# Attention's one-hot rows, AV groups and background steps rearranged in a fused attention and two-layer MoE kernel

## The chip, the cores and the metric

The kernel runs on one core of a Trainium2 chip. The metric is device time of one execution in microseconds (us); lower is better. The engines are PE (TensorE), DVE (VectorE), ACT (ScalarE), POOL (GpSimd) and SP (SyncE, which here only issues DMAs); each works through its own queue in the order in which the built program puts it.

## The reference

Sixteen heads (2 batches of 8) of 768 tokens and 64 dimensions. Every query and key is assigned to one of 16 centroids of its head; a score counts only where both have the same one. The result goes through two mixture-of-experts layers.

```python
q_assign = np.argmax(np.einsum('bhsd,hcd->bhsc', q_n, c_n), axis=-1)
k_assign = np.argmax(np.einsum('bhsd,hcd->bhsc', k_n, c_n), axis=-1)
mask = q_assign[:, :, :, None] == k_assign[:, :, None, :]
scores = scale * np.matmul(q, k.transpose(0, 1, 3, 2))
scores = np.where(mask, scores, -1000000000.0)
attn = np.exp(scores - np.max(scores, axis=-1, keepdims=True))
attn = attn / (np.sum(attn, axis=-1, keepdims=True) + 1e-09)
return np.matmul(attn, v)
```

Then `x` (1536 rows of 512) passes a layer whose tokens with `x @ w_skip > 0` go to the best of 8 experts, and a second layer in which all tokens do, each with an output gate. Expert weights are 512x1024 and 1024x512.

## The kernel before

**Attention**, from about 20 to 305 us of the span, is what the change touches. Heads are numbered 0 to 15 here, and each has six blocks `i` of 128 queries. The loop over `steps` does for block `i` of head `t`: the scores and the maximum of the block after it (`score`), its exponentials (`probs`), the work that belongs to this `i`, and the six transposes of its own exponentials (`flips`), which go through two PSUM tiles `tp` to the SBUF tile `PT`.

- `score` (L450 to 462) is four matmuls into one of two PSUM tiles `s`: two with QA and KA (L455), two with QB and KB (L457), then the negated row maximum on DVE (L461). QB and KB have 80 rows: 64 of data, and in rows 64 to 79 the one-hot assignment, which makes the mask by an added large negative number. So the second pair of a head's first score needs that head's one-hot rows.
- `dots`, `dots_sum` and `cluster` make the assignment of a later head: small matmuls into the free quarter of a `tp` tile (L420), their sums on DVE (L427), five small DVE steps (`first_max`). `one_hot` (L435) turns the result, 128 tokens by 16 clusters for each of six token groups, into rows by six transposes (L442) for the queries and six for the keys, and ACT copies them (L446, L448) into rows 64 to 79 of QB and KB.
- `av` (L479) multiplies `PT` with the values, six matmuls for each half of a head (three blocks). Matmul `k` writes 64 rows of the PSUM tile `o`, even `k` the lower and odd `k` the upper ones. `merge` (L491) projects and scales the half; after the last head of a batch it also writes 2 x 768 KB of rows to DRAM (L516).
- `load` and `split` fetch a head and split it into two parts; the split is five POOL instructions (L403 to L407).
- `split_weights` (L121) splits one eighth of the first expert's weights in each of heads 1 to 8: a copy on ACT (L135), and a subtraction on DVE (L138) when `flush_late` is called.
- `bg.step(2)` runs two steps of the generators that route batch 0 while batch 1 is in attention (heads 8 and later), small DVE instructions and a few matmuls.

The order on each engine is not the program's own: in attention a scheduler places the instructions by readiness and priority when the program is built, and the engines then keep that order. The MoE part behind attention is scheduled by hand and is not touched.

Of the kernel before, what the change touches and what calls it, by code (L numbers as in the profile page):

```python
# [35 lines left out]
def as32(ap):  # L36
    return ap.bitcast(F32)
# [3 lines left out]
def fused_kernel(ctx: ExitStack, tc: tile.TileContext, qT, kT, v, cN, wg, w11, w12, w21, w22, out):  # L41
    nc = tc.nc
    X = nc.dram_tensor("x_rows", (N, DM), F32, kind="Internal").ap()
    X2 = nc.dram_tensor("x2_rows", (N, DM), F32, kind="Internal").ap()

    const = ctx.enter_context(tc.tile_pool(name="const", bufs=1))
    wA = ctx.enter_context(tc.tile_pool(name="wA", bufs=1))
# [24 lines left out]
    def late_constants(pool):  # L72
        nc.gpsimd.memset(onesb, 1.0)
        nc.gpsimd.affine_select(out=trib, in_=onesb, pattern=[[1, 128]], compare_op=ALU.is_gt, fill=0.0, base=0, channel_multiplier=-1)
        for t in (TB1, TB2, base1, base2, LG2):
            nc.gpsimd.memset(t, 0.0)
        nc.sync.dma_start(out=wg2, in_=wg[:, 9:25].rearrange("(c p) g -> p c g", p=128))
        return (iota_f(pool, "io128", 128, [[1, 128]], 0, 0), iota_f(pool, "io12", NA, [[1, NA]], 0, 0),
                iota_f(pool, "d8", E, [[-1, E]], E, 0), iota_f(pool, "tok1", NA, [[128, NA]], 1, 1))
# [31 lines left out]
    def flush_late():  # L111
        for fn in [late.pop(0) for _ in range(len(late))]:
            fn()
# [273 lines left out]

    def split(t):

        if t >= NH:  # L390
            return
        qp, kp, vp = raw.pop(t)
        QA = spl.tile([128, S], F32R, tag="QA", name="QA")
        KA = spl.tile([128, S], F32R, tag="KA", name="KA")
        QB = spl.tile([80, S], F32R, tag="QB", name="QB")
        KB = spl.tile([80, S], F32R, tag="KB", name="KB")
        if t == 0:
            nc.scalar.copy(out=KA[:], in_=kp)
# [30 lines left out]
    def cluster(t, n):  # L429
        if t >= NH:  # L430
            return
        for _ in range(n):
            next(clus[t][0])

    def one_hot(t, s):  # L435
        if t >= NH:
            return
        oh = clus[t][1]
        T = ops[t][2 + s]
        po = ps_o.tile([80, S], BF16, tag="o", name="po") if s == 0 and t == 0 else ps_m.tile([80, S], BF16, tag="misc", name="po")  # L440
        for j in range(NJ):
            nc.tensor.transpose(out=po[64:80, 128 * j:128 * j + 128], in_=oh[:, s * NJ + j], identity=identb)  # L442
        if s == 0 and t == 0:
            nc.vector.tensor_copy(out=T[64:80], in_=po[64:80])
        elif s == 0:
            nc.scalar.copy(out=T[64:80], in_=po[64:80])  # L446
        else:
            nc.scalar.activation(out=T[64:80], in_=po[64:80], func=AF.Copy, scale=BIG, bias=-BIG)  # L448

    def score(t, i):  # L450
        QA, KA, QB, KB, _ = ops[t]
        sl = slice(128 * i, 128 * i + 128)
        s = ps_s.tile([128, S], F32, tag="s", name="s")
        for n0, n1 in ((0, 512), (512, S)):
            nc.tensor.matmul(out=s[:, n0:n1], lhsT=QA[:, sl], rhs=KA[:, n0:n1], start=True, stop=False)  # L455
        for n0, n1 in ((0, 512), (512, S)):
            nc.tensor.matmul(out=s[:, n0:n1], lhsT=QB[:, sl], rhs=KB[:, n0:n1], start=False, stop=True)  # L457
        if i == 0:
            sums[t] = asm.tile([128, NJ], F32, tag="rs", name="rs", bufs=2)
        mx = asm.tile([128, 1], F32, tag="mx", name="mx", bufs=4)  # L460
        nc.vector.tensor_reduce(out=mx, in_=s, axis=AX.X, op=ALU.max, negate=True)  # L461
        return s, mx

    def probs(t, i, s, mx):
        pr = prb.tile([128, S], F32, tag="pr", name="pr")
        nc.scalar.activation(out=pr, in_=s, func=AF.Exp, bias=mx, accum_out=sums[t][:, i:i + 1])  # L466
        return pr

    def flip(i, pr, PT, c):
# [90 lines left out]
    nc.vector.tensor_tensor(out=chl[:, :, 1], in0=c3, in1=as32(chl[:, :, 0]), op=ALU.subtract)  # L560

    split(0)
    load(1)
    split(1)
    d16 = iota_f(asm, "d16", NCL, [[-1, NCL]], NCL, 0)
    load(2)
    for c in (2, 1, 0):
        dp = ps_t.tile([128, 4, 128], F32, tag="tp", name="dp0")[:, 0].rearrange("p (t s) -> p t s", t=4)
        dots(0, c, dp)
        dots_sum(0, c, dp)  # L570
    cluster(0, 5)
    one_hot(0, 1)
    one_hot(0, 0)


    G = asm.tile([128, H, D + NG], F32, name="G")
    for p in (LO, HI):
        nc.sync.dma_start(out=G[p, :, D:], in_=wg.rearrange("(h d) g -> d h g", d=D))
        nc.gpsimd.tensor_scalar(out=G[p, :, 0:D], in0=ident[p, p].unsqueeze(1).to_broadcast([64, H, D]), scalar1=1.0, scalar2=1.0, op0=ALU.mult, op1=ALU.mult)
    io128, io12, d8, tok1 = late_constants(asm)  # L580

    wsets = [w_tiles(wA, "A"), None]
    wdone = 0
    def flips(t, i, pr, hook=None):

        for c in range(2):
            tp, dst = flip(i, pr, PT[t, i // 3], c)
            if hook and c == 0:
                hook(tp)
            if c == 0 or i % 2 == 0:  # L590
                nc.scalar.copy(out=dst, in_=tp[:, 0:3])  # L591
            else:
                nc.vector.tensor_copy(out=dst, in_=tp[:, 0:3])

    steps = [(t, i) for t in range(NH) for i in range(NJ)]
    cur = score(0, 0)
# [6 lines left out]
    for g, (t, i) in enumerate(steps[:-1]):  # L603
        half = i // 3
        if i % 3 == 0:
            PT[t, half] = ptb.tile([128, NJ, 384], F32, tag="PT", name="PT")
        old = pr
        cur = score(*steps[g + 1])
        pr = probs(*steps[g + 1], *cur)
        if i == 0:  # L610
            if t:
                av(t - 1, 1, PT[t - 1, 1], 0, 4)
            load(t + 3)
            split(t + 2)
            cluster(t + 1, 1)
        elif i == 1:
            if t:
                av(t - 1, 1, PT[t - 1, 1], 4, 6)
            cluster(t + 1, 1)
        elif i == 2:  # L620
            if t == NH - 1:
                first_turn()
            if t:
                merge(t - 1, 1)
                if t == H:
                    bg.add(route1(lg[0], 0, ps_m, asm, None, 2))
                    bg.add(first_tile())
                    bg.add(route_skip(lg[0], tok1[:, 0:NJ], ps_m, asm, 2))
            cluster(t + 1, 1)
        elif i == 3:  # L630
            one_hot(t + 1, 0)
            av(t, 0, PT[t, 0], 0, 2)
            if 1 <= t <= 8:
                if t == 1:
                    fetch(False, 2)
                split_weights(t - 1, False, False)
        elif i == 4:
            flush_late()
            one_hot(t + 1, 1)
            av(t, 0, PT[t, 0], 2, 6)  # L640
        elif i == 5:
            merge(t, 0)

        def hook(tp):
            if i > 2 and t + 2 < NH:
                dp = tp[:, 3].rearrange("p (t s) -> p t s", t=4)
                dots(t + 2, i - 3, dp)
                dots_sum(t + 2, i - 3, dp)

        flips(t, i, old, hook)  # L650
        if i == 0 or i == 1:
            cluster(t + 1, 1)
        if i > 1:
            bg.step(2)
    bg.drain()
    tl = NH - 1

# [621 lines left out]
```

## Time and profile before

| | |
|---|---|
| median of 3 runs | 724.88 us (724.53 to 724.91) |
| profiled execution | 725.64 us, span 723.9 us |
| mean granted TensorE clock | 0.969 |
| PE busy | 661.9 us (91%) |
| DVE busy | 464.0 us (64%) |
| ACT busy | 416.0 us (57%) |
| POOL busy | 185.2 us (26%) |

The span is the time from the first to the last instruction of the profiled execution; its own time is 1.7 us more. PE's matmuls overlap in the records, so the time that a group takes is best read as the start of the next group less its own start. A float32 matmul of four passes has two records, so that "x4" at an AV group is two matmuls of the program.

### The profile page before, as it was taken

Reading aid. Unit: us, or ns where it says so; the run is one execution under the profiler, and the core shown is the slowest. Engines: PE = TensorE matmul, PEld = TensorE weight load, DVE = VectorE, ACT = ScalarE, POOL = GpSimd, SP = SyncE. Lnnn points to the kernel's source line nnn. Section 1 sums busy time; section 2 is a strip of 40 time slices with the busy share of each in tenths; the row PEclk is TensorE's granted clock in tenths of the full one; section 3 lists DMA queues with packets and bytes.
Section 4 is the critical chain, followed back from the end, with each engine's and each line's share of the span. In section 5 each row is a group of like instructions: output and inputs, shape, how many; then the busy total and the mean of one; then the engine's idle time right before and its main releaser. Section 6 shows DMA issues by size and latency. Waiting matters only on the chain. (4 is left out here: it accounts for less than half of the span.)

```text
span 723.9 us, 12161 instructions
## 1 busy us (share of the span) xinstructions
PE 661.9 (91%) x4346; PEld 528.3 (73%) x4346; DVE 464.0 (64%) x964; ACT 416.0 (57%) x801; POOL 185.2 (26%) x193
## 2 busy tenths in 40 slices
PE   3999999998999999988988987988997999999995
PEld 2776667766667776766876876876875888899784
DVE  4667766668776667448767797857645755665520
ACT  1678877776566677535546766545534755555420
POOL 5544344433224310104211211201032022103011
PEclk9999999999899999989999999898899999999999
DMA  6747533347123102156637887727634576666200
GB/s 170 177 114 175 168 106 90 87 123 226 42 55 102 26 3 91 71 210 202 225 96 272 279 263 273 227 75 275 199 126 153 178 262 235 221 196 223 70 7 29
DMA packets 46554, 110.78 MB, mean 153 GB/s; under 512 B 7218, under 2 KB 9266, under 8 KB 46448
## 3 DMA queue, kind: packets, MB, share of 16 engines
q1 hardware_dynamic: 41536, 95.60, 42.5%
q0 software_dynamic: 4912, 13.88, 5.9%
q8 instruction: 52, 0.85, 0.5%
q14 instruction: 54, 0.44, 0.2%
HBM read 92.05 MB, written 13.24 MB: 145 GB/s over the span
## 5 line engine op out<-in xcount | busy, mean ns | idle before, releaser
L461 DVE TENSOR_REDUCE mx<-s 128x1 f32<-128x768 f32 x96 | 91.6, 955 | 30.7 <-PE s L457 26.9
L466 ACT ACTIVATE pr<-s,mx 128x768 f32<-128x768 f32 x96 | 86.8, 905 | 32.0 <-DVE mx L461 31.2
L473 PE MATMUL tp<-ident,pr 128*128 128x128 f32 x576 | 94.7, 289 | 5.0 <-ACT PT L591 4.4
L473 PEld LDWEIGHTS tp<-ident,pr 128*128 128x128 f32 x576 | 63.8, 145 | 42.7 <-ACT PT L591 18.5
L485 PE MATMUL o<-PT,vp 128*64 128x384 f32 x384 | 83.2, 512 | 0.2
L591 ACT COPY PT<-tp 128x384 f32<-128x384 f32 x144 | 65.7, 480 | 30.3 <-PE tp L473 23.6
L681 POOL DMA_INDIRECT xg<-x_rows,gi x33 | 38.8, 1177 | 110.6 <-DVEq L1134 39.2
L455 PE MATMUL s<-KA,QA 128*128 128x512 f32 x192 | 60.8, 393 | 3.6 <-DVE QA L401 3.4
L705 PE MATMUL ph<-w1hA,xt 128*128 128x256 f32 x208 | 54.1, 324 | 8.6 <-DVEq L1134 4.9
L457 PE MATMUL s<-KB,QB 80*128 80x512 f32 x192 | 53.4, 356 | 1.1 <-ACT KB L448 1.1
L705 PE MATMUL py<-w2hA,hh 128*128 128x512 f32 x112 | 47.9, 428 | 2.8 <-DVE hh L779 2.8
L705 PE MATMUL py<-w2hB,hh 128*128 128x512 f32 x112 | 46.6, 416 | 3.4 <-DVE hh L779 3.4
L705 PEld LDWEIGHTS ph<-w1hA,xt 128*128 128x128 f32 x208 | 40.4, 214 | 12.7 <-issue 10.4
L705 PE MATMUL ph<-w1hB,xt 128*128 128x256 f32 x192 | 43.8, 300 | 4.8 <-DVEq L1134 2.3
L705 PE MATMUL py<-w2lA,hh 128*128 128x512 f32 x112 | 47.5, 424 | 0.0
L705 PE MATMUL py<-w2lB,hh 128*128 128x512 f32 x112 | 46.3, 413 | 0.0
L817 DVE SCALAR_TENSOR_TENSOR hl<-phw,hh 128x256 fp32r<-128x256 f32 x48 | 20.2, 421 | 35.7 <-ACT hh L816 35.7
L485 PEld LDWEIGHTS o<-PT,vp 128*64 128x64 f32 x384 | 23.6, 138 | 25.6 <-issue 18.5
L338 DVE TENSOR_TENSOR xt<-tp,xt 128x512 fp32r<-128x512 f32 (+1 forms) x32 | 21.8, 681 | 29.6 <-ACT xt L337 25.2
L705 PE MATMUL ph<-w1lA,xt 128*128 128x256 f32 x128 | 40.4, 336 | 0.0
L816 ACT ACTIVATE hh<-phw 128x256 fp32r<-128x256 f32 x48 | 18.5, 385 | 37.5 <-PE phw L705 36.1
L138 DVE TENSOR_TENSOR w2lA<-raw,w2hA 128x1024 fp32r<-128x1024 f32 x32 | 39.1, 1227 | 0.2 <-ACT w2hA L135 0.2
(237 smaller groups left out, 1692.9 us busy)
## 6 DMA issues: line engine op xcount, KB each, us to landing
raw<-w SPq DMA_DIRECT2D x128, 512.0 KB
kp<-kT SPq DMA_DIRECT2D x32, 192.0 KB
qp<-qT SPq DMA_DIRECT2D x32, 192.0 KB
x_rows<-xb SPq DMA_DIRECT2D x8, 768.0 KB
vp<-v SPq DMA_DIRECT2D x16, 192.0 KB
KB<-KA SPq DMA_DIRECT2D x16, 192.0 KB
QB<-QA SPq DMA_DIRECT2D x16, 192.0 KB
xg<-x_rows,gi POOLq DMA_INDIRECT x33, 5.1
```

Of the source, the lines that this page charges most:

```text
L138: nc.vector.tensor_tensor(out=lo, in0=src, in1=as32(hi), op=ALU.subtract)
L338: nc.vector.tensor_tensor(out=lo, in0=tp, in1=as32(hi), op=ALU.subtract)
L455: nc.tensor.matmul(out=s[:, n0:n1], lhsT=QA[:, sl], rhs=KA[:, n0:n1], start=True, stop=False)
L457: nc.tensor.matmul(out=s[:, n0:n1], lhsT=QB[:, sl], rhs=KB[:, n0:n1], start=False, stop=True)
L461: nc.vector.tensor_reduce(out=mx, in_=s, axis=AX.X, op=ALU.max, negate=True)
L466: nc.scalar.activation(out=pr, in_=s, func=AF.Exp, bias=mx, accum_out=sums[t][:, i:i + 1])
L473: nc.tensor.transpose(out=tp[:, kk], in_=pr[:, 128 * k:128 * k + 128], identity=ident)
L485: nc.tensor.matmul(out=po[r:r + 64, :], lhsT=vp[:, k, :], rhs=PT[:, k, :], start=(k < 2), stop=(k >= NJ - 2))
L591: nc.scalar.copy(out=dst, in_=tp[:, 0:3])
L681: nc.gpsimd.indirect_dma_start(out=xg, out_offset=None, in_=src, in_offset=bass.IndirectOffsetOnAxis(ap=gi, axis=0))
L705: nc.tensor.matmul(**kw)
L817: nc.vector.scalar_tensor_tensor(out=ht[1][:, f, :], in0=ph, scalar=0.0, in1=as32(ht[0][:, f, :]), op0=ALU.max, op1=ALU.subtract)
```

## The change

1. One-hot rows. `one_hot` (for heads 1 to 15) now makes two transposes, one for queries and one for keys, each of 128 tokens by all 96 columns (6 groups x 16 clusters). ACT copies both into an SBUF tile `st`; one DMA writes `st` to a DRAM buffer, and two DMAs read it back into rows 64 to 79 of QB and KB. All three are in SP's queue. Head 0 keeps six and six (`one_hot0`).
2. The cluster steps are taken earlier, two at block 0, two at block 1, the last at block 2 together with `one_hot`.
3. AV is asked for as one group of six per half, at block 1 and block 4, where it was 4 and 2, and 2 and 4.
4. `behind` runs a piece of the program with an ordering edge: its DVE instructions are queued behind the newest block's maximum, and its ACT instructions behind that block's exponentials. It is order only, no wait. The weight splits and the background steps go through it, the latter now at every block.
5. The sums of the dots are placed behind the copy of their `tp` tile, and the loads of heads 1 and 2 and the split of head 1 behind head 0's one-hot rows.

```diff
-    def one_hot(t, s):
+    def one_hot(t):
...
+        oh = clus[t][1].rearrange("p j c -> p (j c)")
+        po = ps_m.tile([NJ * NCL, 2, 128], BF16, tag="misc", name="po")
+        st = asm.tile([NJ * NCL, 2, 128], F32R, tag="st", name="st", bufs=2)
+        for s in range(2):
+            nc.tensor.transpose(out=po[:, s], in_=oh[:, NJ * NCL * s:NJ * NCL * (s + 1)], identity=identb)
+        nc.scalar.copy(out=st[:, 0], in_=po[:, 0])
+        nc.scalar.activation(out=st[:, 1], in_=po[:, 1], func=AF.Copy, scale=BIG, bias=-BIG)
+        slot = OH[t % 2]
+        nc.sync.dma_start(out=slot.rearrange("s r t -> r s t"), in_=as32(st[:]))
+        for s in range(2):
+            nc.sync.dma_start(out=as32(ops[t][2 + s][64:80]).rearrange("c (j t) -> c j t", j=NJ), in_=slot[s].rearrange("(j c) t -> c j t", c=NCL))
+    def behind(fn):
+        with tc.issue_after(paced["DVE"]), tc.issue_after(paced["ACT"]):
+            fn()
...
-        nc.vector.tensor_reduce(out=mx, in_=s, axis=AX.X, op=ALU.max, negate=True)
+        paced["DVE"] = nc.vector.tensor_reduce(out=mx, in_=s, axis=AX.X, op=ALU.max, negate=True).ins
...
     split(0)
-    load(1)
-    split(1)
     d16 = iota_f(asm, "d16", NCL, [[-1, NCL]], NCL, 0)
-    load(2)
...
     io128, io12, d8, tok1 = late_constants(asm)
+    load(1)
+    split(1)
+    load(2)
...
         if i == 0:
-            if t:
-                av(t - 1, 1, PT[t - 1, 1], 0, 4)
             load(t + 3)
             split(t + 2)
-            cluster(t + 1, 1)
+            cluster(t + 1, 2)
         elif i == 1:
             if t:
-                av(t - 1, 1, PT[t - 1, 1], 4, 6)
-            cluster(t + 1, 1)
+                av(t - 1, 1, PT[t - 1, 1], 0, 6)
+            cluster(t + 1, 2)
...
             cluster(t + 1, 1)
+            one_hot(t + 1)
         elif i == 3:
-            one_hot(t + 1, 0)
-            av(t, 0, PT[t, 0], 0, 2)
             if 1 <= t <= 8:
                 if t == 1:
                     fetch(False, 2)
-                split_weights(t - 1, False, False)
+                behind(lambda: split_weights(t - 1, False, False))
         elif i == 4:
-            flush_late()
-            one_hot(t + 1, 1)
-            av(t, 0, PT[t, 0], 2, 6)
+            behind(flush_late)
+            av(t, 0, PT[t, 0], 0, 6)
...
-        flips(t, i, old, hook)
-        if i == 0 or i == 1:
-            cluster(t + 1, 1)
-        if i > 1:
-            bg.step(2)
+        flips(t, i, old, hook, after)
+        behind(lambda: bg.step(2))
```

What it makes of the built order stands at three places. Numbers at the names count tiles; they differ between the two programs.

PE, the second half's AV group of a head (tile `o`, L485 before and L505 now), at the change to the next head. Before:

```order
L455 MATMUL s_1651<-KA_1185,QA_1184 128x512
L455 MATMUL s_1651<-KA_1185,QA_1184 128x256
L485 MATMUL o_1613<-PT_1487,vp_736 64x384 x4
L473 MATMUL tp_1639<-ident_61,pr_1575 128x128 x3
L473 MATMUL tp_1644<-ident_61,pr_1575 128x128 x3
L457 MATMUL s_1651<-KB_1187,QB_1186 128x512
L457 MATMUL s_1651<-KB_1187,QB_1186 128x256
L485 MATMUL o_1613<-PT_1487,vp_736 64x384 x2
```

PE, the same place now:

```order
L493 MATMUL tp_1556<-ident_61,pr_1496 128x128 x3
L475 MATMUL s_1562<-KA_1152,QA_1151 128x256
L505 MATMUL o_1613<-PT_1461,vp_717 64x384
L477 MATMUL s_1525<-KB_1154,QB_1153 128x512
L477 MATMUL s_1525<-KB_1154,QB_1153 128x256
L477 MATMUL s_1562<-KB_1154,QB_1153 128x512
L477 MATMUL s_1562<-KB_1154,QB_1153 128x256
L505 MATMUL o_1613<-PT_1461,vp_717 64x384 x5
```

The six matmuls stand as one and five, where they stood as four and two. The one-hot rows are first needed by the second pair of `s_1525`. Over the whole program the groups of AV were 28 of two, 28 of four, 9 of one and 5 of three matmuls; now they are 27 of one, 27 of five, 3 of six, 2 of three and one each of two and four.

DVE, at block 4 of one of heads 1 to 8 (L138 and L139 are the weights' subtraction, `dt` the sums of the dots, which free a `tp` tile). Before:

```order
L461 TENSOR_REDUCE mx_1272<-s_1267 128x1
L427 TENSOR_REDUCE dt_1296<-tp_1288 128x64
L138 TENSOR_TENSOR w2lA_268<-raw_1757,w2hA_267 128x1024
L593 COPY PT_1266<-tp_1300 128x3x128
L461 TENSOR_REDUCE mx_1310<-s_1305 128x1
L427 TENSOR_REDUCE dt_1296<-tp_1331 128x64
```

DVE, the same place now:

```order
L613 COPY PT_1461<-tp_1484 128x3x128
L481 TENSOR_REDUCE mx_1494<-s_1489 128x1
L139 TENSOR_TENSOR w2lA_268<-raw_1071,w2hA_267 128x1024
L428 TENSOR_REDUCE dt_1480<-tp_1472 128x64
L428 TENSOR_REDUCE dt_1480<-tp_1510 128x64
L517 RECIPROCAL rr_1644<-rr_1644 128x3
```

The first sum of the dots now stands behind the maximum of the head's last block and behind the subtraction; all eight subtractions stand so. The block's transposes into `tp_1510` use the buffer that this sum frees, and on PE they stand right behind the first half's group of five.

SP, at the end of batch 0 (head 8), where `x_rows` and `x2_rows` are the 768 KB writes of `merge`, and `one_hot` the rows of head 9:

```order
L536 DMA x_rows<-xb_470 128x3x512
L536 DMA x2_rows<-xb_470 128x3x512
L459 DMA one_hot<-st_2087 96x2x128
L385 DMA qp_2226<-qT 64x768 x2
L461 DMA QB_1795<-one_hot 16x6x128
L461 DMA KB_1796<-one_hot 16x6x128
```

Before, this queue had no one-hot rows. In other heads the three DMAs stand together.

## Rows read from the trace of the kernel before

**Rows 1.** Windows: stretch, its length, busy time of each engine, PEclk, DMA share, GB/s.

```profile
140.00:160.00 20.00, 20.00 (x150) 15.23 (x149) 12.90 (x29) 14.26 (x34) 9.94 (x10) 1.00 0.37 97
...
168.00:171.00 3.00, 3.00 (x24) 2.01 (x22) 2.35 (x10) 2.95 (x8) 0.17 (x1) 1.00 0.93 345
```

**Rows 2.** Timeline of PE: start, duration, line, operation; one-hot transposes and AV groups.

```profile
100.59 0.50 PE L442 MATMUL po<-identb,oh 128*16 128x128 bf16 x6
101.03 0.86 PE L485 MATMUL o<-PT,vp 128*64 128x384 f32 x2
101.82 0.55 PE L473 MATMUL tp<-ident,pr 128*128 128x128 f32 x3
...
111.33 1.51 PE L485 MATMUL o<-PT,vp 128*64 128x384 f32 x8
112.77 0.87 PE L473 MATMUL tp<-ident,pr 128*128 128x128 f32 x6
...
113.69 0.87 PE L485 MATMUL o<-PT,vp 128*64 128x384 f32 x4
114.49 0.87 PE L473 MATMUL tp<-ident,pr 128*128 128x128 f32 x6
```

**Rows 3.** Timeline of PE: the first half's merge in heads 7 to 10, and a wait.

```profile
158.10 0.80 PE L500 MATMUL pf<-G,ot 128*128 128x89 f32 x6
...
174.72 0.80 PE L500 MATMUL pf<-G,ot 128*128 128x89 f32 x6
178.16 0.90 PE L473 MATMUL tp<-ident,pr 128*128 128x128 f32 x3 [2.63 <-ACT PT L591]
...
198.27 0.80 PE L500 MATMUL pf<-G,ot 128*128 128x89 f32 x6
...
218.46 0.80 PE L500 MATMUL pf<-G,ot 128*128 128x89 f32 x6
```

**Rows 4.** Timelines of POOL and DVE in the routing of head 8.

```profile
175.53 1.79 POOL L407 TENSOR_TENSOR QA<-qp,QA 64x768 fp32r<-64x768 f32 x1
...
175.66 1.74 DVE L286 TENSOR_TENSOR gz<-lg,goh 128x48 f32<-128x48 f32 x1
```

**Rows 5.** Timeline of PE: a score's first pair with its second half apart.

```profile
32.25 0.48 PE L455 MATMUL s<-KA,QA 128*128 128x512 f32 x1
32.56 0.51 PE L420 MATMUL tp<-chl,QA 128*128 128x32 f32 x4
```

**Rows 6.** Timelines of PE and DVE: a score, its maximum; a subtraction and a sum.

```profile
164.99 0.59 PE L455 MATMUL s<-KA,QA 128*128 128x512 f32 x2
165.42 0.52 PE L457 MATMUL s<-KB,QB 80*128 80x512 f32 x2
...
165.97 0.96 DVE L461 TENSOR_REDUCE mx<-s 128x1 f32<-128x768 f32 x1
...
87.15 1.53 DVE L138 TENSOR_TENSOR w2lA<-raw,w2hA 128x1024 fp32r<-128x1024 f32 x1
88.97 0.29 DVE L427 TENSOR_REDUCE dt<-tp 128x64 f32<-128x128 f32 x1 [0.29 <-PE tp L420]
```

**Rows 7.** Group of lines by form: the subtraction of the first weight matrix, set A.

```profile
L138 DVE TENSOR_TENSOR w1lA<-raw,w1hA 128x1024 fp32r<-128x1024 f32 x32 | 38.5, 1217 | 0.6 <-ACT w1hA L135 0.4
```

**Rows 8.** Timelines of SP and its waiters: two transfers from issue to use.

```profile
0.82 0.39 SPq L539 DMA_DIRECT2D c<-cN  x1
...
2.52 0.61 DVE L542 TENSOR_TENSOR csq<-c 128x64 f32<-128x64 f32 x1 [2.52 <-DMA c<-cN]
...
8.44 0.59 SPq L384 DMA_DIRECT2D kp<-kT  x1
...
11.99 0.84 POOL L403 TENSOR_SCALAR KA<-kp 128x768 fp32r<-128x768 f32 x1 [6.71 <-DMA kp<-kT]
```

**Rows 9.** Timeline of PE at the start: what stands ahead of the first transposes.

```profile
20.76 1.29 PE L420 MATMUL dp<-chl,QA 128*128 128x32 f32 x6
...
23.31 1.54 PE L473 MATMUL tp<-ident,pr 128*128 128x128 f32 x6
```

More of the change, by code (lines that the diff above doesn't have):

```diff
@@ L44, in fused_kernel @@
     X2 = nc.dram_tensor("x2_rows", (N, DM), F32, kind="Internal").ap()
+    OH = nc.dram_tensor("one_hot", (2, 2, NJ * NCL, 128), F32, kind="Internal").ap()
     const = ctx.enter_context(tc.tile_pool(name="const", bufs=1))
@@ L433, in cluster, with one_hot0 @@
             next(clus[t][0])
-    def one_hot(t, s):
+    def one_hot0(s):
+        oh = clus[0][1]
+        T = ops[0][2 + s]
+        po = ps_o.tile([80, S], BF16, tag="o", name="po") if s == 0 else ps_m.tile([80, S], BF16, tag="misc", name="po")
+        for j in range(NJ):
+            nc.tensor.transpose(out=po[64:80, 128 * j:128 * j + 128], in_=oh[:, s * NJ + j], identity=identb)
+        if s == 0:
+            nc.vector.tensor_copy(out=T[64:80], in_=po[64:80])
+        else:
+            nc.scalar.activation(out=T[64:80], in_=po[64:80], func=AF.Copy, scale=BIG, bias=-BIG)
+    def one_hot(t):
         if t >= NH:
             return
[L438 to L448, printed above, removed]
+        oh = clus[t][1].rearrange("p j c -> p (j c)")
[9 more added lines that the diff above has]
+            nc.sync.dma_start(out=as32(ops[t][2 + s][64:80]).rearrange("c (j t) -> c j t", j=NJ), in_=slot[s].rearrange("(j c) t -> c j t", c=NCL))
+    paced = {}
+    def behind(fn):
+        with tc.issue_after(paced["DVE"]), tc.issue_after(paced["ACT"]):
+            fn()
     def score(t, i):
@@ L465, in probs @@
         pr = prb.tile([128, S], F32, tag="pr", name="pr")
-        nc.scalar.activation(out=pr, in_=s, func=AF.Exp, bias=mx, accum_out=sums[t][:, i:i + 1])
+        paced["ACT"] = nc.scalar.activation(out=pr, in_=s, func=AF.Exp, bias=mx, accum_out=sums[t][:, i:i + 1]).ins
         return pr
@@ L571, in fused_kernel @@
     cluster(0, 5)
-    one_hot(0, 1)
-    one_hot(0, 0)
+    one_hot0(1)
+    one_hot0(0)
     G = asm.tile([128, H, D + NG], F32, name="G")
@@ L580, in fused_kernel, with flips @@
     io128, io12, d8, tok1 = late_constants(asm)
+    load(1)
+    split(1)
+    load(2)
     wsets = [w_tiles(wA, "A"), None]
     wdone = 0
-    def flips(t, i, pr, hook=None):
+    def flips(t, i, pr, hook=None, after=None):
         for c in range(2):
@@ L593, in flips @@
                 nc.vector.tensor_copy(out=dst, in_=tp[:, 0:3])
+            if after and c == 0:
+                after(tp)
     steps = [(t, i) for t in range(NH) for i in range(NJ)]
@@ L635, in fused_kernel, with after @@
                     fetch(False, 2)
-                split_weights(t - 1, False, False)
+                behind(lambda: split_weights(t - 1, False, False))
         elif i == 4:
-            flush_late()
-            one_hot(t + 1, 1)
-            av(t, 0, PT[t, 0], 2, 6)
+            behind(flush_late)
+            av(t, 0, PT[t, 0], 0, 6)
         elif i == 5:
             merge(t, 0)
+        dp = []
         def hook(tp):
             if i > 2 and t + 2 < NH:
-                dp = tp[:, 3].rearrange("p (t s) -> p t s", t=4)
-                dots(t + 2, i - 3, dp)
-                dots_sum(t + 2, i - 3, dp)
-        flips(t, i, old, hook)
-        if i == 0 or i == 1:
-            cluster(t + 1, 1)
-        if i > 1:
-            bg.step(2)
+                dp.append(tp[:, 3].rearrange("p (t s) -> p t s", t=4))
+                dots(t + 2, i - 3, dp[0])
+        def after(tp):
+            if dp:
+                dots_sum(t + 2, i - 3, dp[0])
+        flips(t, i, old, hook, after)
+        behind(lambda: bg.step(2))
     bg.drain()
```

## The prediction

> **What bounds the kernel now.** I read the windows first. In the steady stretch of attention PE is busy all 20.00 of 20 us, while DVE, ACT and POOL have slack [rows 1]; so every microsecond of matmul time put in or taken out counts there, and DVE counts only where PE waits for it. Then PE's timeline, for what its groups cost. The AV matmuls write alternating halves of one tile, and the starts show that neighbours run side by side: a group of one takes 101.82 − 101.03 = .79 us, a group of two 114.49 − 113.69 = .80, a group of four 112.77 − 111.33 = 1.44 (x8 records) [rows 2]. A group therefore costs about .15 plus .64 for each started pair; what counts is where groups are cut. Then the same timeline for waits. From one merge to that of the next head it is 174.72 − 158.10 = 16.62 us, in the next two heads 23.55 and 20.19 [rows 3]; those are heads 8 and 9, where the routing of batch 0 sets in. There PE waited 2.63 us for a copy of exponentials at 178.16 [rows 3], at a time when a routing instruction on DVE, tiny in size, took 1.74 us beside a POOL instruction of 1.79 that began just before it [rows 4].
>
> **AV.** The built order asks for 6 per half but gets 27 groups of one and 27 of five. Before: 28 x .80 + 28 x 1.44 + 9 x .79 + 5 x 1.43 = 77.0 us (three priced like four). Now: 27 x .79 + 27 x 2.08 + 3 x 2.08 + 2 x 1.43 + .80 + 1.44 = 88.8. No row shows five or six; 2.08 is my estimate, 1.44 + .64. **+11.8 us.** A lone matmul and a fifth one have no partner, and PE has no slack there to hide it. The one row for a lone matmul has transposes behind it; now the scores of the next head stand there, so its price lies between .15 and .79. I take .79, the measured one.
>
> **One-hot rows.** Thirty groups of six transposes at 101.03 − 100.59 = .44 us [rows 2] go: 13.2 us. Fifteen groups of two come, each at least .15 (a group's overhead above) and at most .44; I take .2, a third of .44 and a little, so 3.0. **−10.2** (−10.9 to −6.6). The two ACT copies take the place of twelve small ones and are covered: ACT has a third of its time free [rows 1].
>
> **Scores.** In the new order some 30 more first or second pairs have their two halves apart, with other work between them. A whole pair takes .43 (164.99 to 165.42 [rows 6]), a first half alone .31 (32.25 to 32.56 [rows 5]), and the second half, with half the columns, .15 (half of .31) to .31; so a cut costs .03 to .19. I take .08: **+2.4** (.9 to 5.7). PE's own work thus grows by 11.8 − 10.2 + 2.4 = 4.0 us.
>
> **Routing steps.** Behind the maximum they no longer delay a block's maximum or the copies that PE waits for. Heads 8 and 9 hold 23.55 + 20.19 − 2 x 16.62 = 10.5 us over the steady period [rows 3]. About 1 of it (an estimate from the routing's few small matmuls) stays. Of the other 9.5, what is late next is the `PT` copy of the same block, for a routing step behind the maximum still stands ahead of it, and a step can still meet POOL's split. I leave 2 (0 to 5): **−7.5**.
>
> **Weights' subtraction.** It now stands between the last block's maximum and the first sum of the dots, and PE's transposes wait for that sum's `tp` buffer. From the start of the score's second pair: .55 to the maximum (165.42 to 165.97), .96 for it, 1.53 for the subtraction beside POOL (87.15), .29 for the sum [rows 6]: 3.33. PE has meanwhile the rest of that pair, .4, and the group of five, 2.08: 2.5. PE waits .8 in each of eight heads: **+6.4**. Without POOL beside it a subtraction takes 1.22 (38.5 us for 32, [rows 7]), so .5 x 8 = 4 below; if it waits out a POOL instruction like that of 1.79 [rows 4], some 1.4 more, 2.2 x 8 = 17.5 above; and nothing, if PE comes to the place later than I think. I take the row at that place.
> The Trainium skill ("SBUF — State Buffer", Who interferes with whom) says that a DVE instruction with two SBUF inputs contends with a GpSimd instruction that reads SBUF, and that the first to issue holds the shared port for its whole duration. The rows' 1.74 beside 1.79 agrees; by the rule each subtraction could cost a whole split step, which would make the sum 11.1 larger.
>
> **One-hot rows through DRAM.** The three DMAs lie in SP's queue, mostly together, ahead of nothing that is urgent in steady heads. Two transfers in a row, each between 2.52 − .82 = 1.7 us and 11.99 − 8.44 = 3.55 from issue to use [rows 8], with transposes .2, copies .5 to 1 (an estimate, no row shows them) and a second issue at .4 to .6 [rows 8]: 4.5 to 8.9 us. In the order, some nine us of PE's work stand between the transposes and the second score pair that needs the rows. So hidden, at **0**, in steady heads; without the cover each head would pay what is missing. Head 9 is different: half of the batch's 2 x 2 row writes stands just ahead, and 4 x 393 KB = 1.57 MB at the 345 GB/s of the busiest window [rows 1] is 4.6 us in front. I take **+3** (0 to 7, the most that a head of [rows 3] lost).
> The Trainium skill ("DMA: Bandwidth & Descriptors", Anatomy of one DMA — SWDGE (gpsimd) path) puts the fixed cost of a transfer at about 2 us, mostly completion, and warns of surprisingly long delays when the target is HBM. No row of this kernel shows such a write being waited for; two such costs alone would be 4, hidden.
>
> **Start.** Dots of 2.55 us stood ahead of the first transposes (20.76 to 23.31 [rows 9]), in time in which PE waited for exponentials anyway. Now a score that needs a free tile stands there, and the split of head 1 on POOL and its loads on SP come later. **+1** (−1.5 if the dots just move out of the way, +3 if they come back in full). The cluster steps moved earlier and the sums behind their copies are covered by DVE's quarter of free time [rows 1]: 0.
>
> **Sum.** 4.0 − 7.5 + 6.4 + 3 + 1 = +6.9. The profiled execution took 725.64, .76 over the median, so 732.5 there, and **731.8 us** as a median.
>
> **Rivals.**
> 1. *PE is never early (faster).* The waits I price (subtraction 6.4, what is left of routing 2, head 9's 3) all rest on how much PE has queued ahead of the waiting matmul. If some 2 us more stand or pile up there, all go: −11.4, so **720.4**. It decides for faster once over 8.4 of the 11.4 are hidden. For it: PE is full in [rows 1], so it tends to arrive late. Against it: DVE's 3.33 is longer than the group of five, and the order has them face to face.
> 2. *It cancels.* Half of that hidden: 726, or no change.
> 3. *The port decides.* Each subtraction meets a split and waits it out: 17.5 for 6.4, **742.9**. For: [rows 4]; against: the 1.53 of [rows 6].
> 4. *The DRAM trip is late in each head.* At 9 us or a little over, plus queued loads, some 1 us x 14: **745.8**. Against: the cover of nine us is at the top of my sum.
> 5. *The lone AV matmul is nearly free*, beside what follows: 27 x .64 = 17.3 less, **714.5**. Against: the lone matmul at 101.03 held up PE's next group for .79 [rows 2].
>
> **Numbers.** Forecast .40, rival 1 .26, rival 2 .10, rival 3 .10, rival 4 .08, rival 5 .06. The range leaves out rivals 4 and 5 and the far half of 3, under 2 in 10: 717 (rival 1 with the start at −1.5 and one-hot at its lower end) to 743. A measurement of this kernel tells about .2%, 1.45 us, from no change. Faster: .26 + .06 = .32; same .10; slower .40 + .10 + .08 = .58. The forecast's own range is 727 to 737.
>
> **What would show it.** AV: starts of groups of five 2.08 apart from the next group, lone ones .79; lone ones under .3 would prove rival 5. Subtraction: eight waits of PE at block 5's transposes, near .8, released by a sum of the dots (none: rival 1; over 2: rival 3). DRAM trip: PE waiting for DMA at the second score pair in head 9 alone (all heads: rival 4). Routing: periods of heads 8 and 9 near 18 instead of 23.55 and 20.19. Steady heads should grow by about (11.8 + 2.4 − 10.2)/15, .3 us, and heads 1 to 8 by .8 more. Steady heads under 16.62 would prove the AV term wrong.

## The result and the profile after

The changed kernel takes 734.2 us (732.51 to 735.88, 4 runs) beside 724.7 (723.02 to 724.91) for the kernel before: 1.0136 times as long, 95% interval 1.0107 to 1.0165. That is slower by 1.4%, clear of the noise, 2.4 us over the forecast of 731.8 and inside its range of 717 to 743. As will be seen, the sum was nearer than its terms were.

The profiled execution after has a span of 731.8 us against 723.9. Where the 7.9 us arise is read from landmarks of PE's timeline, the start of the first half's merge of a head in each kernel:

| landmark | before | after | grown by, since the one above |
|---|---|---|---|
| first merge, head 0 | 37.28 | 38.28 | +1.0 |
| head 1 | 54.26 | 61.02 | +5.8 |
| head 8 | 174.72 | 185.77 | +4.3 |
| head 10 | 218.46 | 224.50 | −5.0 |
| head 14 | 287.20 | 297.37 | +4.1 |
| first MoE matmul | 305.66 | 314.75 | −1.1 |
| end of the span | 723.9 | 731.8 | −1.2 |

A steady head (6 to 7) now takes 167.83 − 149.88 = 17.95 us, where it took 16.62 [rows 3]. PE's timeline after, in such heads, with the same columns as [rows 2]:

```profile
133.99 0.86 PE L505 MATMUL o<-PT,vp 128*64 128x384 f32 x2
134.78 0.97 PE L477 MATMUL s<-KB,QB 80*128 80x512 f32 x4
135.68 2.15 PE L505 MATMUL o<-PT,vp 128*64 128x384 f32 x10
137.76 0.88 PE L493 MATMUL tp<-ident,pr 128*128 128x128 f32 x6
...
142.74 0.40 PE L477 MATMUL s<-KB,QB 80*128 80x512 f32 x1
142.97 0.28 PE L455 MATMUL po<-identb,oh 128*96 128x128 bf16 x2
143.06 0.36 PE L477 MATMUL s<-KB,QB 80*128 80x256 f32 x1
...
149.88 0.35 PE L520 MATMUL pf<-G,ot 128*128 128x89 f32 x2
...
167.83 0.80 PE L520 MATMUL pf<-G,ot 128*128 128x89 f32 x6
```

The lone AV matmul holds PE for 134.78 − 133.99 = .79 us, though scores and not transposes stand behind it; the five take 137.76 − 135.68 = 2.08; the two transposes 143.06 − 142.97 = .09. Adding all such differences of starts by kind of group, in one steady head before and after (worked out from the whole timeline):

| group | before | after | |
|---|---|---|---|
| AV | 4.48 | 5.74 | +1.26 |
| one-hot transposes | .86 | .08 | −.78 |
| scores | 5.05 | 5.75 | +.70 |
| merge | 1.28 | 1.46 | +.18 |
| the rest | 4.95 | 4.92 | −.03 |

The prediction had a steady head grow by some .3 us, and by .8 more in heads 1 to 8 for the subtraction. It grew by 1.33, none of it the subtraction's, as PE's waits below show. Yet in the kernel before heads 1 to 3, each from its first merge to the next head's, took 17.67, 18.53 and 18.36 and not 16.62, so that from head 1 to head 8 only 4.3 us came in all.

The five largest rows of PE's waits after, from the view of waits between 20 and 310 us (engine, tile and line, what it waited for: us in all, times, longest):

```profile
PE tp L493 <- ACT pr L486: 2.7, 4, 1.7
PE s L475 <- ACT pr L486: 1.4, 1, 1.4
PE pr L221 <- DVE gohm L217: 0.8, 1, 0.8
PE po L455 <- DVE xb L532: 0.6, 1, 0.6
PE pf L520 <- ACT ot L508: 0.6, 1, 0.6
```

No row of that view has PE waiting for a sum of the dots (`dt`): the eight waits behind the subtraction, which the prediction priced at 6.4 us, do not exist. PE's two waits for `PT` in heads 8 and 9, 2.63 [rows 3] and 1.77, are gone. ACT shows the other end of that stall. Before, from the same view:

```profile
ACT PT L591 <- DVE dt L427: 6.4, 5, 3.0
...
PE tp L473 <- ACT PT L591: 4.4, 2, 2.6
```

Two of ACT's five waits, 2.59 and 3.01 us, lie in heads 8 and 9: its copies stood behind sums of the dots, and those stood on DVE behind routing steps. After, no such line is left. That by itself is the work of part 5, which places the sum behind the copy: the line is absent without the edge on the steps too (e4), and with that edge but without part 5 (e6) 1.9 us of it stay, the longest .6.

The new loss sits between heads 0 and 1. PE's timeline after, there:

```profile
40.33 2.16 PE L505 MATMUL o<-PT,vp 128*64 128x384 f32 x12
43.06 0.90 PE L520 MATMUL pf<-G,ot 128*128 128x89 f32 x6 [0.58 <-ACT ot L508]
44.56 0.31 PE L455 MATMUL po<-identb,oh 128*96 128x128 bf16 x2 [0.59 <-DVE xb L532]
44.68 0.95 PE L477 MATMUL s<-KB,QB 80*128 80x512 f32 x4
47.34 1.54 PE L493 MATMUL tp<-ident,pr 128*128 128x128 f32 x6 [1.72 <-ACT pr L486]
```

The second pairs of two scores of head 1 (44.68) stand behind six AV matmuls, a whole merge and the transposes of head 2's one-hot rows. Nothing is then left to do while the exponentials run, PE waits three times, and the clock falls behind that. Windows, columns as in [rows 1]:

```profile
44.00:48.00 4.00, 1.72 (x9) 1.36 (x10) 2.32 (x4) 2.14 (x6) 0.00 (x0) 0.81 0.37 67
48.00:52.00 4.00, 4.00 (x18) 3.71 (x17) 1.47 (x2) 2.29 (x6) 0.00 (x0) 0.50 1.03 326
```

From 48 to 52 PE was granted .50, the 1.2 GHz level. The rows themselves were not late. The DMA issues of the page, median us from issue to landing at the end of each line:

```profile
one_hot<-st SPq DMA_DIRECT2D x15, 96.0 KB, 1.7
QB<-one_hot SPq DMA_DIRECT2D x15, 48.0 KB, 2.0
KB<-one_hot SPq DMA_DIRECT2D x15, 48.0 KB, 2.1
```

Head 1's last issue, from SP's timeline, was eight us ahead of 44.68:

```profile
36.19 0.43 SPq L461 DMA_DIRECT2D KB<-one_hot  x1
```

What is late is the place that the order gives to the scores.

### The profile page after: what moved, and what is told of

It reads as the page before. It is cut to its first block, busy times and chain, and to the rows that moved or that the text cites. A ratio compares the mean times of both kernels' runs of the same rounds, so it can differ in the third digit from the quotient of the medians.

```text
span 731.8 us, 11917 instructions
## 1 busy us (share of the span) xinstructions
PE 664.9 (91%) x4196; PEld 526.5 (72%) x4196; DVE 462.4 (63%) x964; ACT 401.2 (55%) x801; POOL 190.7 (26%) x193
## 5 line engine op out<-in xcount | busy, mean ns | idle before, releaser
L505 PE MATMUL o<-PT,vp 128*64 128x384 f32 x384 | 93.1, 499 | 0.6
L493 PEld LDWEIGHTS tp<-ident,pr 128*128 128x128 f32 x576 | 66.0, 146 | 35.9 <-ACT pr L486 12.5
L475 PE MATMUL s<-KA,QA 128*128 128x512 f32 x192 | 64.8, 404 | 4.7 <-DVE QA L402 3.1
L725 PE MATMUL ph<-w1hA,xt 128*128 128x256 f32 x208 | 52.0, 313 | 8.7 <-DVEq L1154 5.2
L505 PEld LDWEIGHTS o<-PT,vp 128*64 128x64 f32 x384 | 29.8, 136 | 35.4 <-issue 30.4
L725 PE MATMUL ph<-w1hB,xt 128*128 128x256 f32 x192 | 46.2, 312 | 9.3 <-PEq L1154 4.2
L613 DVE COPY PT<-tp 128x384 f32<-128x384 f32 x48 | 26.8, 557 | 29.1 <-PE tp L493 27.8
L725 PEld LDWEIGHTS ph<-w1hB,xt 128*128 128x128 f32 x192 | 35.5, 208 | 11.8 <-issue 10.2
L139 DVE TENSOR_TENSOR w1lA<-raw,w1hA 128x1024 fp32r<-128x1024 f32 x32 | 39.8, 1257 | 2.8 <-ACT w1hA L136 2.7
L136 ACT CAST w1hA<-raw 128x1024 fp32r<-128x1024 f32 x32 | 33.0, 1045 | 14.2 <-PEq L1154 6.2
```

The costliest lines, as they stand in the source:

```text
L136: nc.scalar.copy(out=hi, in_=src)
L139: nc.vector.tensor_tensor(out=lo, in0=src, in1=as32(hi), op=ALU.subtract)
L493: nc.tensor.transpose(out=tp[:, kk], in_=pr[:, 128 * k:128 * k + 128], identity=ident)
L505: nc.tensor.matmul(out=po[r:r + 64, :], lhsT=vp[:, k, :], rhs=PT[:, k, :], start=(k < 2), stop=(k >= NJ - 2))
L725: nc.tensor.matmul(**kw)
```

## The experiments

All ratios are to the kernel before, run beside it on the same chip, with a 95% interval. Six experiments start from the changed kernel (e1 to e5, e8), the others from the kernel before. "Head 6 takes" means the time from head 6's first merge to head 7's.

**e1, AV asked for one block earlier.**

```diff
         if i == 0:
+            if t:
+                av(t - 1, 1, PT[t - 1, 1], 0, 6)
...
-            if t:
-                av(t - 1, 1, PT[t - 1, 1], 0, 6)
...
         elif i == 3:
+            av(t, 0, PT[t, 0], 0, 6)
...
-            av(t, 0, PT[t, 0], 0, 6)
```

> The changed kernel with AV asked for one block earlier (block 0 and block 3, one call of six each). In the built order 29 of the 34 groups are now six matmuls, where the changed kernel has 27 of one and 27 of five. Theory (a cut at an odd place costs a whole .64 slot): AV takes 29 x 2.08 + .79 + .80 + 2 x 1.43 + 1.44 + 2.08 = 68.3 us instead of 88.8, so about 20 us off the changed kernel, near 714 us, steady heads near 16.6 us. Rival (lone matmuls run beside their neighbours, and the changed kernel is long for another reason): under 4 us off, near 731. Second rival (PE reaches the group before PT is copied): waits on ACT or DVE copies of PT take the 20 us back.

Measured: 728.7 us, 1.0059 (1.0028 to 1.0089): some 5 us better than the change and not 20. Steady heads take 17.35. PE's timeline:

```profile
139.37 0.58 PE L520 MATMUL pf<-G,ot 128*128 128x89 f32 x4
140.29 0.87 PE L493 MATMUL tp<-ident,pr 128*128 128x128 f32 x6 [0.34 <-ACT pr L486]
...
141.97 2.52 PE L505 MATMUL o<-PT,vp 128*64 128x384 f32 x12
144.42 0.55 PE L493 MATMUL tp<-ident,pr 128*128 128x128 f32 x3
...
148.81 0.62 PE L475 MATMUL s<-KA,QA 128*128 128x512 f32 x2 [0.29 <-ACT pr L486]
```

The uncut six take 144.42 − 141.97 = 2.45, not 2.08, and two new waits for exponentials, .34 and .29, stand in each steady head. AV fell from 5.74 to 4.98 a head, where two uncut groups at 2.08 would be 4.16. A group placed this early runs into copies that are not done (one of its weight loads waits .18 for ACT's copy of `PT`, at 142.98), and no longer stands where PE would have waited for exponentials; much of what was saved in slots came back as waits, as the second rival said in kind.

**e2, head 1's one-hot rows on the chip.** `one_hot_on` is the kernel before's function.

```diff
-            one_hot(t + 1)
+            if t:
+                one_hot(t + 1)
+            else:
+                one_hot_on(1, 0)
+                one_hot_on(1, 1)
```

> The changed kernel with the one-hot rows of head 1 alone turned as before (six and six transposes, no DRAM trip). Theory (the 5.8 us that the stretch from head 0's to head 1's first merge grew come from head 1's rows being planned late by the scheduler, so that AV, merge and head 2's transposes stand ahead of head 1's first scores and PE runs dry): that stretch falls from 22.74 to about 17.8, the kernel by 4 to 5 us, near 729.5. Rival (the loss comes from the later load and split of head 1): the stretch stays at 22 to 23 and the kernel within 1.5 us of 734.

Measured: 729.5 us, 1.0062 (1.0029 to 1.0095), 5 less than the change, as expected. The stretch fell from 22.74 to 15.98, further than to 17.8, but head 0's first merge came 1.7 later (39.97) and the next stretch grew from 17.12 to 19.05. PE was granted 1.00 from 40 to 64 us. So the loss between heads 0 and 1 was the trip's, by way of the order; net of the two shifts, 3.1 us of it are back at head 2's first merge (75.00 instead of 78.14), and the rest of the 5 comes later.

**e3, the weight splits without the edge.**

```diff
-                behind(lambda: split_weights(t - 1, False, False))
+                split_weights(t - 1, False, False)
...
-            behind(flush_late)
+            flush_late()
```

> The changed kernel without the ordering edge on the weight splits (copy and subtraction placed by the scheduler as before). The prediction's term (PE waits .8 us in each of eight heads behind the subtraction): 6 us off, near 728. Rival from the trace after (PE shows no wait there, the transposes that follow use the other tp buffer): within 1.5 us of 734, up to the cuts of AV, 25 groups of one and 25 of five, about 1 us less.

Measured: 735.7 us, 1.0146 (1.0079 to 1.0214), no different from the change. Taking the edge away gains nothing: heads 2 and 3 become longer (18.47 and 18.56, where they took 17.93 and 17.94). The prediction's term falls. One subtraction meets POOL here as the third rival feared, in DVE's and POOL's timelines:

```profile
97.39 1.84 POOL L408 TENSOR_TENSOR QA<-qp,QA 64x768 fp32r<-64x768 f32 x1
...
97.95 2.36 DVE L139 TENSOR_TENSOR w2lA<-raw,w2hA 128x1024 fp32r<-128x1024 f32 x1
```

It takes 2.36 us beside a usual 1.22, with POOL's instruction begun .56 ahead of it.

**e4, the background steps without the edge.**

```diff
-        behind(lambda: bg.step(2))
+        if i > 1:
+            bg.step(2)
```

> The changed kernel without the ordering edge on the background steps, taken at blocks 2 to 5 as before. Theory (the edge removed the stall of heads 8 and 9, 7.5 us): about 7 us more, near 741, with heads 8 and 9 together near 46 us instead of 38.7 and PE waiting for a PT copy there. Rival (the stall went because other changes moved DVE's work): within 1.5 us of 734.

Measured: 738.1 us, 1.0162 (1.0105 to 1.0218). Its interval overlaps the change's, so by the time alone this is not settled. In the trace heads 8 and 9 take 24.39 + 16.84 = 41.2 us instead of 38.7, and PE waits there 1.07 for a sum of the dots, 1.54 and .60 for exponentials. The direction is the theory's, a third of its size. Part 5, which is in this kernel, takes ACT's copies from behind the sums as well; that this is why so little comes back is argued, not shown.

**e5, all one-hot rows on the chip.** The call of `one_hot` goes, `one_hot_on(t + 1, 0)` stands at block 3 and `one_hot_on(t + 1, 1)` at block 4.

> The changed kernel with all one-hot rows turned on the chip again, six and six transposes per head at blocks 3 and 4 (AV still cut, 26 groups of one and 26 of five). Theory (the DRAM trip saves PE .78 us in each steady head and costs 5.8 once, in head 1): 14 x .78 = 11 more and 5.8 less, about 5 us over the changed kernel, near 739; steady heads near 18.7 us, the stretch between the first merges of heads 0 and 1 near 18. Rival (the trip costs PE something in steady heads too, as the cuts of the score beside it): steady heads stay at 17.9 and the kernel is 5 us faster, near 729.

Measured: 726.2 us, 1.0027 (1.0000 to 1.0054): 8 us better than the change, where the theory had 5 worse. Steady heads take 18.15, only .2 more than with the trip. The transposes cost .86 instead of .08, but scores and merge give back .64 of that. So the trip is worth .2 us a head on PE, not .78, and costs more than that in head 1 (22.74, here 18.31) and in heads 8 and 9 (36.5 instead of 38.7). By the first MoE matmul 4.0 us are gained; the rest of the 8 lies behind it, where the order is the same.

**e6, the kernel before with the edge on the background steps.** `paced` and `behind` as in the change, and:

```diff
-        if i > 1:
-            bg.step(2)
+        behind(lambda: bg.step(2))
```

> The kernel before with the ordering edge on the background steps alone, taken at every block (AV 29 groups of two and 29 of four, 6 of one, 4 of three). Theory (this edge alone removes the stall of heads 8 and 9): 7.5 us off the kernel before, .990, with heads 8 and 9 together near 36 us instead of 43.7. Rival (the edge only moves the wait, and other parts of the change removed it): within .2 % of the kernel before.

Measured: 711.3 us, **.9821** (.9771 to .9871). Heads 8 and 9 take 17.28 + 17.50 = 34.8 us, 9.0 less than before. This part alone is worth more than the 7.5 that the prediction gave it. It holds two things, the edge and the steps at six blocks of a head instead of four, and no run has one without the other.

**e7, the kernel before with both edges.** e6 and:

```diff
-                split_weights(t - 1, False, False)
+                behind(lambda: split_weights(t - 1, False, False))
...
-            flush_late()
+            behind(flush_late)
```

> The kernel before with the ordering edge on the background steps and on the weights' split. The built order has AV in 31 groups of two and 32 of four, no lone one left but two. Theory (lone AV matmuls cost a slot, the subtraction behind the maximum costs PE nothing): AV 2 x .79 + 31 x .80 + 32 x 1.44 = 72.5 instead of 77.0, so 4.5 more off than with the edge on the steps alone, about 12 us under the kernel before, .984. The prediction's term (subtraction .8 in each of eight heads): 6.4 longer than that, .992.

Measured: **703.4 us, .9691 (.9646 to .9736)**, faster than both kernels and than either theory. All heads from 2 to 7 take 16.62 or 16.63; before, those from 1 to 4 took 17.67, 18.53, 18.36 and 16.04. All of PE's waits above the view's threshold between 20 and 300 us:

```profile
PE tp L480 <- ACT pr L473: 0.6, 3, 0.2
PE s L462 <- ACT pr L473: 0.2, 1, 0.2
PE pf L507 <- ACT ot L495: 0.2, 1, 0.2
```

And DVE at the place that the prediction feared, in head 7:

```profile
150.17 0.96 DVE L468 TENSOR_REDUCE mx<-s 128x1 f32<-128x768 f32 x1
151.05 1.53 DVE L138 TENSOR_TENSOR w2lA<-raw,w2hA 128x1024 fp32r<-128x1024 f32 x1
152.88 0.29 DVE L427 TENSOR_REDUCE dt<-tp 128x64 f32<-128x128 f32 x1 [0.29 <-PE tp L420]
```

The sum waits for PE, not PE for the sum.

**e8, parts joined to the change.** e2, the old place of load and split of head 1, AV's first half in 2 and 4, and its second half with an edge to the newest score's last matmul:

```diff
+                with tc.issue_after(paced["PE", t, 2]):
+                    av(t - 1, 1, PT[t - 1, 1], 0, 6)
...
         elif i == 3:
+            av(t, 0, PT[t, 0], 0, 2)
...
-            av(t, 0, PT[t, 0], 0, 6)
+            av(t, 0, PT[t, 0], 2, 6)
```

> The changed kernel with head 1's one-hot rows turned on the chip, the load and split of head 1 where they were, and AV's second half queued behind the last score matmul of the block before it, its first half in two and four: 17 groups of two, 17 of four, 14 of six, one each of one and five. Theory: AV .79 + 17 x .80 + 17 x 1.44 + 2.08 + 14 x 2.08 = 70.1 instead of 88.8, head 1's 5 us and the start's 1 us come back, so 20 to 24 us off the changed kernel, near 712, about .983 of the kernel before. Rival (with PE quicker, the exponentials and copies become what each block waits for, as .6 us a head with uncut groups of six): 8 to 12 us off, near 724, the same as the kernel before.

Measured: 746.2 us, 1.0297 (1.0248 to 1.0346), 34 us over what was expected. PE's timeline:

```profile
136.39 0.85 PE L490 MATMUL s<-KB,QB 80*128 80x512 f32 x4
139.16 0.87 PE L506 MATMUL tp<-ident,pr 128*128 128x128 f32 x6 [1.92 <-ACT pr L499]
...
140.22 0.52 PE L490 MATMUL s<-KB,QB 80*128 80x512 f32 x2
140.67 2.16 PE L518 MATMUL o<-PT,vp 128*64 128x384 f32 x12
```

AV's second half is uncut here (2.09 for six), and PE stands idle for 1.92 us ahead of it, once in each steady head: two scores end together, and the group that could have filled the time of their maxima and exponentials is queued behind the next score. In every second steady head, though not in the others, PE's granted clock falls soon after this pause, to .50 from 122 to 124 us, and the six matmuls that start at 121.61 hold PE for 3.37 us. Windows of two heads, columns as in [rows 1]:

```profile
97.36:115.16 17.80, 15.88 (x113) 11.59 (x111) 12.15 (x26) 11.85 (x28) 7.55 (x8) 1.00 0.51 119
115.16:134.55 19.39, 17.48 (x112) 12.10 (x111) 12.12 (x25) 11.84 (x28) 7.54 (x8) 0.91 0.49 109
```

AV's matmuls are the filler between a score and its transposes; in this kernel where they stand counts for more than how they are cut.

**e9, e7 with AV asked for as one call.** Part 3 of the change on e7.

> The kernel of e7 (before with both edges) with AV asked for as one call of six per half at blocks 1 and 4, the change's part 3 alone. In the built order 16 groups of one, 16 of five, 15 of six, one each of two and four. Theory (AV's price is read from its cuts alone): 16 x .79 + 31 x 2.08 + .80 + 1.44 = 79.4 instead of 72.5 us, so 7 us over e7, near 710.5. Rival (a lone matmul is nearly free): within 1.5 us of e7, 703.

Measured: 707.5 us, .9760 (.9713 to .9807), 4 to 5 over e7 where 7 were expected. Steady heads take 17.01 instead of 16.62, and AV 4.96 instead of 4.48 in them: the cuts are the cost, by the price that was read before.

**e10, e7 with the trip through DRAM** for heads 2 to 15, with the cluster steps as in the change (parts 1 and 2).

> The kernel of e7 with the one-hot rows of heads 2 to 15 turned in two transposes and placed by DMA, cluster steps as early as in the change; head 1 on the chip, AV asked for as before. Its built order has AV in 12 groups of one, 17 of two, 6 of three, 18 of four, 10 of five, one of six. Theory (the trip itself makes the scheduler cut AV and the scores, since the second score pair is planned after the trip's landing): 14 x .78 = 11 us of transposes less, 8 more for AV's cuts (80.5 instead of 72.5), about 7 more for cut scores, so 3 to 5 over e7, near 707. Rival (the trip is a gain by itself and only AV's one call hurts): 8 to 11 under e7, near 694.

Measured: 717.8 us, .9907 (.9878 to .9935), 14 over e7, more than either had it. In heads 5 to 7 the trip gains .05 us (16.56 and 16.57 for 16.62): transposes −.79, AV +.63, scores +.1. Heads 1 to 3 take 18.4, with cut groups and a wait of 1.21 for exponentials in two of them; heads 8 and 9 take 18.69 and 18.61 (17.23 and 17.52 in e7), and there a DMA is waited for, once:

```profile
178.68 0.94 PE L480 MATMUL s<-KB,QB 80*128 80x512 f32 x4 [0.19 <-DMA KB<-one_hot]
```

**e11, the kernel before with the edge on the weight splits alone.** e7 without its edge on `bg.step`.

> The kernel before with the ordering edge on the weights' split alone. AV 30 groups of two, 31 of four, 5 of one, one of three: 74.0 us instead of 77.0. Theory (the subtraction behind the maximum costs PE nothing, and without it between score and sum heads 1 to 4 lose their cuts, 17.0 to 18.5 becoming 16.6): 5 to 6 off the kernel before, .993, with the stall of heads 8 and 9 as it was. The prediction's term: 6.4 more than the kernel before, 1.009.

Measured: 716.2 us, .9877 (.9833 to .9920), where the prediction's term would make it 1.009. Heads 1 to 7 take 16.98, 16.62 and so on, as in e7; the stall of heads 8 and 9 stays (22.30 + 20.19).

**e12, e7 with part 5 of the change** (sums behind the copies, later loads and split).

> The kernel of e7 with the change's part 5 (sums of the dots placed behind the copy of their tile, loads of heads 1 and 2 and split of head 1 behind head 0's one-hot rows). Its AV groups are 31 of two, 31 of four, 3 of one, one of three. Theory (this part costs what the start lost before head 0's first merge, 1.0 us, and nothing in steady heads): within 1.5 us of e7, .969 to .972 of the kernel before. Rival (this part is where the change's remaining loss lies, some 10 us that the edges, AV's one call and the trip do not add up to): .98 or more.

Measured: 708.3 us, .9778 (.9727 to .9830), from .1 hundredths under to 1.8 over e7's .9691 by the ends of the intervals taken crosswise, so that the times alone do not quite settle it. In the trace head 0's first merge comes at 41.02 instead of 36.95, and heads 9, 10 and 12 take .4 to .7 more, with waits of PE for a copy on DVE. By the first MoE matmul it is 6.6 us behind e7. So part 5 costs some 6 us, not 1, most of it at the start.

## Why the prediction was right, and where it was not

**The sum held because errors cancelled.** The parts come to: both edges −22 us (e7, on the kernel before), and on top of that, one at a time, AV's one call +5 (e9), the trip with the earlier cluster steps +16 (e10), part 5 +6 (e12), by ratios times 724. Their sum is +5, and the change measured +9.9. By the first MoE matmul of the profiles the same parts are −14.2, +3.3, +9.1 and +6.6, in all 4.8, and the change 9.1. e10 leaves out the trip of head 1, which e2 puts at some 5 us; that would close the gap. But each interval is some 2 to 4 us to either side, and the parts act on each other (27 lone AV matmuls where e9 had 16 and e10 12), so what is left is not shown to be anything.

- **AV, +11.8.** Right in mechanism and price: .79 and 2.08 are what the rows after show, +1.26 a steady head. e9 measures +5 for this part alone, with 16 lone ones. Not all 27 of the change come from its one call, nor from the trip: e5, without the trip, still has 26. The idea that uncutting them in the change gives all of it back fell (e1, e8).
- **One-hot rows, −10.2.** The transposes did fall by 9.99 us between the first merges of heads 1 and 14. But the step "hidden, at **0**, in steady heads" was wrong. The landing was indeed hidden: in steady heads no line of PE's waits names a DMA. The place in the order was not. With the trip in the program, AV and scores are cut elsewhere (e10: AV +.63 a head), and e5 finds .2 us a head left of .78. That the scheduler reckons with a late landing is the likely reason, and no run shows it. The copies to ACT were also read wrongly: two replaced two, not twelve small ones, at .25 and .29 us where they were .79 and .80.
- **Scores, +2.4.** Too small: .70 a steady head, 6.8 over heads 1 to 13. Cuts and waits too short to be marked on the page are both in it, and were not told apart.
- **Routing steps, −7.5.** Right place and nearly the size: e6 takes 9.0 off heads 8 and 9. In the change heads 8 and 9 are 2 x 17.95 + 2.8, so 7.7 of the 10.5 us over the steady period went, with head 9's trip in the same stretch. The edge is not alone in that: part 5 took ACT's copies from behind the sums, which the prediction priced at 0.
- **Weights' subtraction, +6.4.** This step failed, and in sign: on the kernel before the edge on it is a gain (e11: .9877), and in the change it costs nothing (e3). The error lies in the statement that PE's next transposes need the `tp` buffer that the sum frees. The trace after has it otherwise, in PE's and DVE's timelines of head 6:

```profile
148.14 0.55 PE L493 MATMUL tp<-ident,pr 128*128 128x128 f32 x3
...
149.55 0.49 PE L493 MATMUL tp<-ident,pr 128*128 128x128 f32 x3
```

```profile
147.04 1.54 DVE L139 TENSOR_TENSOR w2lA<-raw,w2hA 128x1024 fp32r<-128x1024 f32 x1
148.51 0.28 DVE L428 TENSOR_REDUCE dt<-tp 128x64 f32<-128x128 f32 x1
```

  The transposes at 148.14 begin before the sum has, so they took the other of the two buffers, whose copy DVE had begun at 145.47; the sum's own is wanted by those at 149.55, 1.4 us later, which is more than the .8 by which it was priced late. What the section on the change says of that buffer is wrong too. What the term also left out is where the scheduler puts a subtraction that is free. In the kernel before all eight stand between 53.52 and 102.96, one of them (78.92) ahead of a maximum (80.53), and heads 1 to 3 around them have AV cut (5.11 to 6.03 us a head instead of 4.48). With the edge they come one to a head, in the same gap behind a maximum, and heads 2 and 3 take 16.6 (e11).
- **Head 9, +3.** The trip was late there as said: its write took 7.3 us to land, the longest of the 15, and PE's weight load waited .6 for the read behind it. But PE had six AV matmuls to run meanwhile: they start at 187.95 and the pair at 190.03, 2.08 later, which is their full price and no gap. So the term was nothing there. The large loss came in head 1 (+5.8), for which the prediction had no term; rival 4 had the trip late "in each head", and it was not late there, only the scores' place was.
- **Start, +1.** The first merge came 1.0 later, but e12 has 4.1 for this part alone.
- **Rivals.** The first (PE never early) was right for the subtraction and for head 9. The third and fifth fell: no subtraction of the change's attention took more than 1.54 us, and the lone matmul cost its full slot.

The rule of the Trainium skill that a two-input DVE instruction contends with a GpSimd instruction that reads SBUF ("SBUF — State Buffer", Who interferes with whom) bore on the stall, and on the subtraction by who began first. In the change DVE begins some .55 us ahead of POOL's split of K in all eight heads; the subtraction takes 1.54 beside a usual 1.22, and POOL's instruction 2.67 where it takes 1.82 elsewhere, off PE's path. In e3, with POOL .56 ahead, the subtraction took 2.36. So the third rival's case exists, at 1.1 us more, and the order of the change kept it away.

**Open.** The span behind the first MoE matmul, where the order is the same in all, was 418.2 us in the kernel before, 417.1 after and 410.5 in e7. Its windows in the kernel before and in e7:

```profile
305.66:723.90 418.24, 375.30 (x2397) 322.78 (x2396) 255.97 (x507) 210.86 (x356) 75.14 (x64) 0.96 0.56 186
```

```profile
291.49:702.00 410.51, 370.57 (x2397) 318.08 (x2396) 255.73 (x507) 211.01 (x357) 75.26 (x64) 0.97 0.58 190
```

Of e7's 22 us, attention explains 14.2 (291.49 against 305.66). The rest does not simply come with a shorter attention: in the fourteen profiled executions this stretch takes 410.5 to 421.0 us, and e8, whose attention is the longest (to 329.27), has 414.3. The granted clock seems to have a part in it: runs of the kernel before alone go from 717.6 to 728.6 us, at mean granted clocks of .984 and .966. How much of the 7.7 is that, no run tells.

## What to carry to other kernels

Split a change into its parts before judging it: this one holds two edges worth 3% together and three parts that cost more than that together, and its total says neither. Where a scheduler makes the order, an operation's price is its own time plus what its place does to the groups around it; count the cut groups in the built order, and ask of each group what it was filling. And before pricing a wait for a buffer, find from the trace which buffer the next user takes.

## What was not expected of the hardware

A write of 96 KB to DRAM and a read of 48 KB landed in 1.7 and 2.0 us in the median of 15, with the longest write at 7.3, queued behind 768 KB writes. The Trainium skill ("DMA: Bandwidth & Descriptors", Anatomy of one DMA — SWDGE (gpsimd) path) warns, for GpSimd's path, of long delays when the target is HBM; here, in SP's queue, the write was the shorter of the two, and its 7.3 in head 9 stood behind other traffic. A pause of 1.92 us on PE was followed in every second steady head of e8 by a fall of the granted clock from 1.00 to .50, and such a head took 1.6 us more. And edges that only order instructions moved the whole kernel by 1.2% (e11) and, together with steps taken at more blocks, by 1.8% (e6), with no work taken out.
